# The first loads of a fused attention and feed-forward kernel: whole transfers for three groups and two weight slices, and another order of the opening

## The chip, the cores and the metric

The kernel runs on one core of one Trainium2 chip. The metric is the device time of one execution in microseconds (us); the median of three runs of the kernel before is 591.53 us (591.43 to 591.8). One more execution was recorded by the hardware profiler.

## The reference

`x` is the output of a chunked attention, and a gated feed-forward layer follows it. Cut to what matters:

```python
# q, k, v: (4, 8, 768, 64); mem_k, mem_v: (4, 8, 8, 64); chunks of 32, 16 to the left, 8 to the right
for c in range(nc):
    k_full = concat([mem_k, k[:, :, l_start:r_end]])      # 8 + up to 56 rows
    v_full = concat([mem_v, v[:, :, l_start:r_end]])
    scores = scale * (q_c @ k_full.T)
    a = exp(scores - max(scores))
    a = a / (sum(a) + 1e-09)
    out[:, :, c_start:c_end] = a @ v_full
x = out.transpose(0, 2, 1, 3).reshape(3072, 512)
h = x @ w_in                                              # (512, 2048)
g = where(h >= 1, h, where(h <= -1, 0, (h + 1) ** 2 / 4))
return g @ w_out                                          # (2048, 512)
```

## The kernel before, in words

The 3072 tokens are done in six blocks of 512. A block's attention output, transposed, is `x` (a high part `xth` and a rest `xtl`); the 2048 hidden units are 16 slices of 128. For a slice, TensorE (PE) multiplies `w_in` and `x` in three products of high and low parts into PSUM (a "hid" step, tile `ps_h`), ScalarE (ACT) and VectorE (DVE) form the gate (`gw`) and split it (`gh`, `gl`), and PE multiplies it by `w_out` into four accumulators (an "out" step, tile `ps_o`).

Weights arrive as raw 64-bit words, 16 pieces of 1024 KB, `w0` to `w15`, and are decoded on the chip by `decode` (line 160): ACT activates (`w`), DVE shifts and ors (`f`), ACT casts the high part, DVE subtracts for the low part (`wr`). The first two, `w0` and `w1`, are decoded in halves (`u0`, `u1` of `w0`; `u2`, `u3` of `w1`); before, each half also comes in a transfer of its own.

The attention of block 0 is done in four groups, g0 to g3 (`first_attention`, line 238). g0 and g1 make up the first 256 tokens, g2 and g3 the others. A group runs: scores on PE (`ps_s`), a mask memset where a window sticks out, maximum (`mx`), subtraction (`pr`), exponential on ACT, sum (`den`), `den + 1e-9`, reciprocal (`rin`), multiplication, four transposes on PE, two copies to `pt` on ACT, values on PE (`ps_x`), cast to `xth` on ACT, subtraction to `xtl` on DVE. g0 takes its maximum and subtraction in two halves; g2 does its exponentials in eight instructions with sums, and g3's scores take the PSUM banks that g2's scores leave. The mask of a group reads the scores of both halves of its queries and keys.

What sets the order around the change is a list written out in the kernel, the string `FIRST` (line 33). Each token advances one chain by one step, and each engine executes in program order. `L5` issues entry 5 of the list `loads` (line 646) on SP's queue; `g`, `u`, `w`, `n` are the chains named above (`n0` to `n3`: attention of later half blocks); `A0` to `A3` are the hid and out steps of slices 0 to 3 for the first 256 tokens, `B0` to `B3` those for the other 256, and `J4` onward the steps for all 512. C, D, E are block 1. The `ps_h` tiles rotate over two PSUM banks, so a hid step or a group's transposes wait until an earlier user of a bank has been read. From block 2 on, a plain loop follows.

Of the kernel before, what the change touches and what calls it, by code (L numbers as in the profile page):

```python
# [30 lines left out]


FIRST = """
    L2 L0 L1 g0 g0 g0 L3 g1 g0 g0 g1 g0 g0 g1 L8 g0 L6 L5 g0 u0 g1 L10 g0 g0 g1 L9 g1 g1 u1 g2 L4 g1
    g1 u1 u0 u0 u2 g0 g2 g0 L12 u0 u0 g2 u2 u1 L13 g3 g2 g1 g0 u1 L7 g2 u2 g2 g0 g3 L11 L16 L14 g3
    L15 L30 g1 u2 g1 L17 g1 g2 g3 L19 A0 g2 A0 g3 g3 g3 u1 u3 g3 A1 A0 L18 g3 w2 g2 g3 u2 g3 u3 u3
    L25 L23 L20 L31 g2 g3 A0 A2 g2 w2 u3 g3 A1 w2 n0 A2 A1 B0 A1 w2 L29 L22 w3 B0 A1 A0 u3 L21 w2 B0
    w3 B0 w5 w3 L28 A2 L27 L26 L24 w3 L32 A0 A1 A3 w5 B1 A3 B0 w5 A3 A2 w3 A2 n0 w5 w4 B1 B1 w4 B0
    B1 B2 A2 B2 B1 B3 B1 B2 J4 B3 n0 n0 w4 w4 B2 A3 n0 w6 B3 w4 A3 B2 n0 J5 w5 A3 B2 B3 w9 J4 w6 J4
    n0 w6 w9 J4 J6 w6 J4 B3 J5 n0 J5 w7 B3 n0 w6 J7 J5 J4 w7 J6 n0 w8 w7 w7 J5 w7 w8 J6 n0 J5 w8 J8  # L40
    w11 J6 J7 J6 J7 w10 w9 n0 w8 J8 n0 n0 w12 w9 J7 J8 w8 w9 J8 J6 n0 n0 w11 w10 n0 J7 n0 w10 w10
    J10 w11 J9 J9 w11 w13 w10 J8 w12 J9 J10 n1 n1 w11 J7 n1 w12 J10 J9 J12 w12 n1 J10 w12 n1 w14 J10
    n1 J9 w14 n1 w14 J8 J11 J9 J12 w13 J12 n1 w14 J11 J12 J13 J11 C0 w15 J12 J13 J11 w13 n1 n1 n1
    L34 L33 n2 J10 J11 n1 w13 C0 C0 w14 n1 J13 n1 C1 n2 C1 n2 n2 n2 C1 w15 C0 C1 J11 w13 J14 n2 J12
    w15 n2 C1 n2 C0 J13 J14 n1 J14 J14 L36 C2 J13 n1 C2 n1 C2 n2 J15 n2 J13 n1 n2 C3 w15 J14 L35 w15
    C2 J15 J14 n2 n2 J15 J15 C2 n2 n2 C3 D0 C3 J15 D1 D0 n2 n2 D1 C3 J15 n3 D0 J15 D1 n2 C3 n2 D2
    J15 n2 J15 D3 C0 C1 D3 D0 D2 n2 D3 n2 D0 D2 n3 n2 E5 D1 D3 n2 D2 E4 C2 n2 D3 D2 D1 E4 J15 E5 E4
    C3 n3 n3 E4 E6 E5 n3 n3 n3 E4 n3 D0 D1 E8 n3 D2 E5 D3 E6 E5 E6 E6 n3 E8 E4 E7 E6 n3 E8 E8 E7 E8
    n3 E5 E6 E7 E9 E10 L38 L37 E9 E7 E7 E9 E10 E10 n3 E7 E9 E9 n3 E13 E8 n3 E10 E12 E9 E10 E10 E12
    n3 E13 E12 n3 E13 E13 E13 E12 E11 E14 E11 E12 n3 n3 E11 n3 E14 E11 n3 E11 E15 E15 E14 E15 L39  # L50
    E11 n3 E12 E14 E14 n3 E15 n3 E15 E13
"""
# [784 lines left out]
```

## Time and profile before

| | |
|---|---|
| median of three runs | 591.53 us |
| profiled execution | 591.96 us |
| its span (first to last instruction) | 590.1 us |
| PE busy | 574.4 us, 97% |
| DVE busy | 332.2 us, 56% |
| ACT busy | 267.7 us, 45% |
| bytes read | 47.84 MB |

The span is what the instructions cover; 1.86 us of the profiled execution lie around it. "Busy" is time in which an engine has an instruction in hand. Every instruction of the kernel carries the line of one helper (L72), so rows are told apart by engine and tile.

### The profile page before, as it was taken

The numbers are of one execution on the slowest core, as the hardware profiler recorded it, in microseconds if no ns is written. First come the engines' busy times: TensorE is split into PE (matmuls) and PEld (weight loads), VectorE is DVE, ScalarE is ACT, GpSimd is POOL, SyncE is SP. The second block draws the span as 40 slices with busy tenths as digits, with TensorE's granted clock in tenths as the row PEclk, the third lists the DMA queues.
The fourth block names the chain that finished last, engine by engine and source line by source line (L and its number), as shares of the span: only waits on it lengthen the run. The fifth ranks groups of instructions, "written<-read, shape, count | busy, mean of one in ns | idle before, by whom it ended". The sixth has DMA issues, their size and how long they took to land.

```text
span 590.1 us, 12043 instructions
## 1 busy us (share of the span) xinstructions
PE 574.4 (97%) x5364; PEld 474.8 (80%) x5364; DVE 332.2 (56%) x489; ACT 267.7 (45%) x468; POOL 2.4 (0%) x7
## 2 busy tenths in 40 slices
...
DMA packets 10709, 54.91 MB, mean 93 GB/s; under 512 B 1185, under 2 KB 1185, under 8 KB 6305
## 3 DMA queue, kind: packets, MB, share of 16 engines
...
q8 instruction: 42, 0.69, 0.5%
...
HBM read 47.84 MB, written 6.29 MB: 92 GB/s over the span
## 4 chain that ended last, share of the span: by engine, by line
PE 85%; DVE 6%; ACT 5%; DMA 1%; issue 1%; SPq 0%; DVEq 0%; ACTq 0%
PE ps_o L72 41%; PE ps_h L72 40%; PE ps_x L72 2%; PE ps_s L72 2%; ACT pr L72 2%; DMA w<-in_first_w_dram 1%; DVE pt L72 1%; DVE f L72 1%; ACT gw L72 1%; ACT f L72 1%; DVE mx L72 1%; DVE gw L72 1%; DVE gl L72 1%; DVE wr L72 1%; ACT w L72 1%
## 5 line engine op out<-in xcount | busy, mean ns | idle before, releaser
L72 PE MATMUL ps_h<-xth,wr 128*128 128x512 f32 (+1 forms) x832 | 195.4, 376 | 1.2 <-ACT pt L72 0.6
L72 PE MATMUL ps_o<-wr,gh 128*128 128x512 f32 x768 | 194.5, 390 | 0.0
L72 PEld LDWEIGHTS ps_h<-xth,wr 128*128 128x128 f32 x832 | 147.5, 188 | 31.6 <-DVE wr L72 0.9
L72 PEld LDWEIGHTS ps_o<-wr,gh 128*128 128x128 f32 x768 | 143.5, 188 | 29.6
L72 DVE SCALAR_TENSOR_TENSOR gw<-ps_h,gw 128x512 f32<-128x512 f32 (+1 forms) x104 | 67.4, 648 | 141.1 <-ACT gw L72 140.4
L72 ACT ACTIVATE gw<-ps_h 128x512 f32<-128x512 f32 (+1 forms) x104 | 58.6, 564 | 178.1 <-PE ps_h L72 173.1
L72 PE MATMUL ps_o<-wr,gl 128*128 128x512 f32 x384 | 106.9, 389 | 0.0
L72 PE MATMUL ps_h<-xtl,wr 128*128 128x512 f32 (+1 forms) x416 | 104.5, 373 | 0.0
L72 DVE TENSOR_TENSOR gl<-gw,gh 128x512 fp32r<-128x512 f32 (+1 forms) x104 | 66.8, 647 | 54.4 <-ACT gh L72 53.8
L72 ACT CAST gh<-gw 128x512 fp32r<-128x512 f32 (+1 forms) x104 | 60.6, 587 | 65.6 <-DVE gw L72 55.6
L72 PEld LDWEIGHTS ps_h<-xtl,wr 128*128 128x128 f32 x416 | 75.0, 188 | 13.9
L72 PEld LDWEIGHTS ps_o<-wr,gl 128*128 128x128 f32 x384 | 72.1, 188 | 15.0
L72 ACT ACTIVATE gw<-gw 128x512 f32<-128x512 f32 (+1 forms) x104 | 62.3, 599 | 3.3
L72 DVE STREAM_TRANSPOSE pt<-pr 32x512 f32<-32x512 f32 (+1 forms) x60 | 41.4, 699 | 1.2
L72 DVE STREAM_TRANSPOSE xt<-xr 32x512 f32<-32x512 f32 (+1 forms) x48 | 33.1, 700 | 6.6 <-ACT xr L72 6.0
L72 ACT ACTIVATE pr<-pr 128x1024 f32<-128x1024 f32 (+1 forms) x12 | 11.4, 952 | 33.2 <-DVE pr L72 33.2
...
L72 DVE COPY ob<-ps_o 128x512 f32<-128x512 f32 (+1 forms) x16 | 9.6, 622 | 23.4 <-PE ps_o L72 23.3
L72 DVE SCALAR_TENSOR_TENSOR f<-w,f 128x1024 uint32<-128x1024 uint32 (+1 forms) x18 | 19.5, 1090 | 3.6 <-ACT f L72 3.4
L72 DVE TENSOR_TENSOR wr<-f,wr 128x1024 fp32r<-128x1024 f32 (+1 forms) x18 | 19.5, 1095 | 1.0 <-ACT wr L72 1.0
L72 ACT CAST wr<-f 128x1024 fp32r<-128x1024 f32 (+1 forms) x18 | 17.0, 951 | 5.9 <-DVE f L72 5.8
...
## 6 DMA issues: line engine op xcount, KB each, us to landing
...
```

The source lines that it names most:

```text
L72: return self.tc.keep_in_program_order(getattr(self.engine, name)(*args, **kwargs))
```

## The change

Groups 1, 2 and 3 get their queries and keys in one transfer each (672 KB) where there were two of 336 KB, and `w0` and `w1` come in one transfer of 1024 KB each where there were two of 512 KB. Group 0 keeps its two halves. Five entries of `loads` become `None`, so the numbers of the others stay. `FIRST` is replaced by another order of the same steps, without the five. `decode` and its halves are as they were.

```diff
 FIRST = """
-    L2 L0 L1 g0 g0 g0 L3 g1 g0 g0 g1 g0 g0 g1 L8 g0 L6 L5 g0 u0 g1 L10 g0 g0 g1 L9 g1 g1 u1 g2 L4 g1
-    g1 u1 u0 u0 u2 g0 g2 g0 L12 u0 u0 g2 u2 u1 L13 g3 g2 g1 g0 u1 L7 g2 u2 g2 g0 g3 L11 L16 L14 g3
-    L15 L30 g1 u2 g1 L17 g1 g2 g3 L19 A0 g2 A0 g3 g3 g3 u1 u3 g3 A1 A0 L18 g3 w2 g2 g3 u2 g3 u3 u3
-    L25 L23 L20 L31 g2 g3 A0 A2 g2 w2 u3 g3 A1 w2 n0 A2 A1 B0 A1 w2 L29 L22 w3 B0 A1 A0 u3 L21 w2 B0
...
+    L0 L1 L2 g0 g0 g0 g0 g1 g0 L5 g0 g1 g0 g0 u0 u0 g1 g1 u1 u0 g0 g0 u0 g1 L8 g1 g1 u1 g1 g0 L10
+    L12 g2 g0 u2 g2 u0 u2 g1 L7 g2 g3 g1 u2 u1 u1 g3 g2 g3 g2 L4 g1 u3 g3 u2 g1 g2 g3 g0 L15 L16 g2
+    g3 g1 g3 L14 g0 g0 L30 g2 g3 u2 u3 L20 u1 A0 g3 g3 w2 g2 g3 L19 u3 w2 A0 A1 A0 g3 g2 L17 A2 L18
+    g3 u3 A1 n0 w2 A2 L22 L23 L24 A0 g2 A2 A1 w6 w2 u3 A0 A1 B0 B0 A0 w5 A2 w2 A3 B0 B1 w3 A2 w5 A1
...
+        if g > 0:
+            sp.dma_start(qk_of[0, g], next_qk[g - 1])
+            return
         at = slice(r * QKF, (r + 1) * QKF)
-        sp.dma_start(qk_of[0, g][:, at], first_qk[g, r])
+        sp.dma_start(qk_of[0, g][:, at], first_qk[r])
...
-    def load_w(i, part=None):
+    def load_w(i):
...
-        if part is None:
-            sp.dma_start(raw[i], w[i - len(SLICED)].bitcast(U32))
-        else:
-            sp.dma_start(raw[i][:, part * n2 : (part + 1) * n2], first_w[i, part].bitcast(U32))
+        sp.dma_start(raw[i], w[i].bitcast(U32))
...
     loads = [
-        (load_first_qk, 0, 0), (load_first_qk, 0, 1), (load_first_qk, 1, 0), (load_first_qk, 1, 1),
-        (load_first_v, 0), (load_w, 0, 0), (load_w, 0, 1), (load_first_v, 1),
-        (load_first_qk, 2, 0), (load_first_qk, 2, 1), (load_w, 1, 0), (load_w, 1, 1),
-        (load_first_qk, 3, 0), (load_first_qk, 3, 1), (load_first_v, 2), (load_first_v, 3),
+        (load_first_qk, 0, 0), (load_first_qk, 0, 1), (load_first_qk, 1, 0), None,
+        (load_first_v, 0), (load_w, 0), None, (load_first_v, 1),
+        (load_first_qk, 2, 0), None, (load_w, 1), None,
+        (load_first_qk, 3, 0), None, (load_first_v, 2), (load_first_v, 3),
     ]
```

In the two orders, VectorE's first instructions are these (the step's name behind the group's, as in the section on the kernel; `shl`, `or`, `lo` are the steps of a decode, `eps` is `den + 1e-9`):

```
before: g0.mx g0.sub g0.mx g0.sub g1.mx g0.den g1.sub g0.eps g0.rin g0.mul g1.den g1.eps g1.rin g1.mul
        u1.shl u0.shl u0.or g2.mx u0.lo u2.shl u1.or g2.eps g2.rin u2.or g2.mul g0.lo g3.mx g3.sub g1.lo
        g3.den g3.eps g3.rin u1.lo g3.mul A0 u2.lo u3.shl u3.or g2.lo w2.shl g3.lo w2.or A1 ...
after:  g0.mx g0.sub g0.mx g0.sub g1.mx g0.den g0.eps u0.shl g1.sub u0.or g0.rin g0.mul g1.den g1.eps g1.rin
        u1.shl g1.mul g2.mx u0.lo u2.shl u2.or u1.or g3.mx g2.eps g3.sub g2.rin g2.mul g3.den g3.eps g1.lo
        g3.rin g0.lo g3.mul u2.lo u3.shl u1.lo u3.or w2.shl A0 g3.lo w2.or g2.lo A2 A1 ...
```

TensorE's, up to the same set of steps done:

```
before: g0 scores, g1 scores, g0 transposes, g2 scores, g1 transposes, g0 values, g3 scores, g1 values,
        g2 transposes, A0 hid, A1 hid, g3 transposes, g2 values, g3 values, A2 hid, n0 scores, B0 hid, ...
after:  g0 scores, g1 scores, g0 transposes, g2 scores, g1 transposes, g3 scores, g1 values, g0 values,
        g2 transposes, A0 hid, g3 transposes, g2 values, g3 values, A1 hid, A2 hid, n0 scores, B0 hid, ...
```

## Rows read from the trace of the kernel before

**Rows 1.** The page: its first line and section 1 (busy time, share of the span, instructions).

```profile
span 590.1 us, 12043 instructions
PE 574.4 (97%) x5364; PEld 474.8 (80%) x5364; DVE 332.2 (56%) x489; ACT 267.7 (45%) x468; POOL 2.4 (0%) x7
```

**Rows 2.** Busy time of the engines by stretch: stretch, its length, busy us (and instructions) of each engine, granted TensorE clock, DMA share, GB/s.

```profile
0.00:28.00 28.00, 17.46 (x396) 12.94 (x396) 18.74 (x42) 16.72 (x40) 2.44 (x7) 1.00 0.95 371
...
33.00:60.00 27.00, 27.00 (x145) 23.04 (x145) 25.92 (x39) 23.44 (x38) 0.00 (x0) 1.00 1.01 421
...
110.00:130.00 20.00, 19.43 (x223) 16.68 (x222) 14.16 (x23) 12.22 (x37) 0.00 (x0) 1.00 0.16 55
130.00:200.00 70.00, 70.00 (x689) 58.45 (x689) 33.36 (x53) 26.80 (x50) 0.00 (x0) 1.00 0.19 69
```

**Rows 3.** The chain that ended last, in order of time: start, duration, what.

```profile
16.59 2.48 ACT pr L72 x16
...
28.12 1.15 PE ps_x L72 x32
29.27 1.63 PE ps_h L72 x12
30.90 1.41 PE ps_s L72 x91
```

**Rows 4.** SP's queue in order of time: start of the issue, duration, tile. From the ninth issue on, SP issues a transfer when the one eight places earlier has landed.

```profile
6.54 0.33 SPq L72 DMA_DIRECT2D qk<-in_first_qk_dram  x1
...
7.87 0.33 SPq L72 DMA_DIRECT2D qk<-in_first_qk_dram  x1
...
9.95 0.33 SPq L72 DMA_DIRECT2D w<-in_first_w_dram  x1
11.22 0.33 SPq L72 DMA_DIRECT2D w<-in_w_dram  x1
...
13.26 1.18 SPq L72 DMA_DIRECT2D v<-in_first_v_dram  x2
...
15.43 0.33 SPq L72 DMA_DIRECT2D qk<-in_qk_dram  x1
...
17.02 0.33 SPq L72 DMA_DIRECT2D w<-in_w_dram  x1
...
19.53 0.33 SPq L72 DMA_DIRECT2D w<-in_w_dram  x1
...
27.81 0.33 SPq L72 DMA_DIRECT2D w<-in_w_dram  x1
```

**Rows 5.** Time from issue to landing of the first transfer (issued at 0.73) and of the second (issued at 1.16), one answer each.

```profile
DMA to landing us min/median/max: 3.1/3.1/3.1
...
DMA to landing us min/median/max: 3.5/3.5/3.5
```

**Rows 6.** Stretches of one microsecond; the last two columns are the DMA share and GB/s.

```profile
4.00:5.00 1.00, 0.32 (x24) 0.32 (x32) 0.00 (x0) 0.00 (x0) 0.00 (x0) 1.00 1.23 328
5.00:6.00 1.00, 0.37 (x31) 0.13 (x11) 0.00 (x0) 0.00 (x0) 0.00 (x0) 1.00 0.73 180
```

**Rows 7.** TensorE in order of time: start, duration, operation, tile, count, and in brackets the idle time before it and what ended it.

```profile
4.68 0.68 PE L72 MATMUL ps_s<-qk 64*32 64x64 f32 x32 [1.61 <-DMA qk<-in_first_qk_dram]
6.56 1.18 PE L72 MATMUL ps_s<-qk 64*32 64x64 f32 x64 [1.19 <-DMA qk<-in_first_qk_dram]
...
12.41 1.08 PE L72 MATMUL ps_h<-ident,pr 128*128 128x128 f32 x4 [3.84 <-DVE pr L72]
...
15.80 1.85 PE L72 MATMUL ps_x<-pt,v 128*64 128x64 f32 x32
19.12 0.86 PE L72 MATMUL ps_s<-qk 64*32 64x64 f32 x64 [1.48 <-ACT pr L72]
21.25 0.66 PE L72 MATMUL ps_h<-ident,pr 128*128 128x128 f32 x4
...
32.24 1.22 PE L72 MATMUL ps_h<-xth,wr 128*128 128x256 f32 x8
```

**Rows 8.** VectorE and ScalarE in order of time, the same columns.

```profile
7.38 0.11 DVE L72 MEMSET ps_s<- 32x64 f32 x1 [6.26 <-PE ps_s L72]
...
9.35 0.69 DVE L72 TENSOR_REDUCE mx<-ps_s 128x8 f32<-128x512 f32 x1
...
9.96 0.68 DVE L72 TENSOR_REDUCE den<-pr 128x8 f32<-128x512 f32 x1
...
11.23 0.66 ACT L72 ACTIVATE w<-w 128x512 f32<-128x512 f32 x1 [1.37 <-DMA w<-in_first_w_dram]
...
11.58 0.69 DVE L72 TENSOR_TENSOR pr<-pr,rin 128x512 f32<-128x512 f32 x1
...
15.61 0.68 DVE L72 TENSOR_REDUCE mx<-ps_s 128x8 f32<-128x512 f32 x1
...
17.12 0.43 DVE L72 TENSOR_SCALAR f<-w 128x512 uint32<-128x512 uint32 x1
...
18.92 1.19 ACT L72 COPY pt<-ps_h 64x512 f32<-64x512 f32 x2
```

**Rows 9.** What TensorE waited for between 100 and 135 us: us in total, times, longest.

```profile
PE ps_h L72 <- DVE gw L72: 0.4, 1, 0.4
PE ps_x L72 <- ACT pr L72: 0.2, 1, 0.2
```

More of the change, by code (lines that the diff above doesn't have):

```diff
@@ L33 @@
 FIRST = """
-    L2 L0 L1 g0 g0 g0 L3 g1 g0 g0 g1 g0 g0 g1 L8 g0 L6 L5 g0 u0 g1 L10 g0 g0 g1 L9 g1 g1 u1 g2 L4 g1
-    g1 u1 u0 u0 u2 g0 g2 g0 L12 u0 u0 g2 u2 u1 L13 g3 g2 g1 g0 u1 L7 g2 u2 g2 g0 g3 L11 L16 L14 g3
-    L15 L30 g1 u2 g1 L17 g1 g2 g3 L19 A0 g2 A0 g3 g3 g3 u1 u3 g3 A1 A0 L18 g3 w2 g2 g3 u2 g3 u3 u3
-    L25 L23 L20 L31 g2 g3 A0 A2 g2 w2 u3 g3 A1 w2 n0 A2 A1 B0 A1 w2 L29 L22 w3 B0 A1 A0 u3 L21 w2 B0
-    w3 B0 w5 w3 L28 A2 L27 L26 L24 w3 L32 A0 A1 A3 w5 B1 A3 B0 w5 A3 A2 w3 A2 n0 w5 w4 B1 B1 w4 B0
@@ L39 @@
[L39 to L48, printed above, removed]
@@ L49 @@
-    n3 E5 E6 E7 E9 E10 L38 L37 E9 E7 E7 E9 E10 E10 n3 E7 E9 E9 n3 E13 E8 n3 E10 E12 E9 E10 E10 E12
-    n3 E13 E12 n3 E13 E13 E13 E12 E11 E14 E11 E12 n3 n3 E11 n3 E14 E11 n3 E11 E15 E15 E14 E15 L39
-    E11 n3 E12 E14 E14 n3 E15 n3 E15 E13
+    L0 L1 L2 g0 g0 g0 g0 g1 g0 L5 g0 g1 g0 g0 u0 u0 g1 g1 u1 u0 g0 g0 u0 g1 L8 g1 g1 u1 g1 g0 L10
+    L12 g2 g0 u2 g2 u0 u2 g1 L7 g2 g3 g1 u2 u1 u1 g3 g2 g3 g2 L4 g1 u3 g3 u2 g1 g2 g3 g0 L15 L16 g2
+    g3 g1 g3 L14 g0 g0 L30 g2 g3 u2 u3 L20 u1 A0 g3 g3 w2 g2 g3 L19 u3 w2 A0 A1 A0 g3 g2 L17 A2 L18
@@ new lines @@
+    g3 u3 A1 n0 w2 A2 L22 L23 L24 A0 g2 A2 A1 w6 w2 u3 A0 A1 B0 B0 A0 w5 A2 w2 A3 B0 B1 w3 A2 w5 A1
+    w3 A3 A1 A3 B1 B0 B2 w3 B0 B1 w4 w3 w5 w3 B0 B3 A3 L25 L21 B2 n0 A2 B3 B1 B2 w4 B2 L26 L32 L27
+    B1 L31 A3 w4 J4 L28 n0 B3 w5 w4 J4 B3 L29 w4 n0 B2 B3 w8 B1 w7 J4 w5 n0 J5 w6 w6 J4 J5 J5 J4 n0
+    w6 B2 w8 n0 w6 J6 J6 B3 A3 J5 J5 w7 J6 w11 w8 w8 J7 J7 n0 w7 n0 J4 J6 w9 J5 n0 n0 w7 w10 J6 w7
+    n0 n0 n0 J8 w10 n0 w8 J7 w12 w10 w9 n0 J7 w9 n0 J7 L33 J9 J9 n0 w9 J9 J6 J8 n1 w9 w10 n1 w10 L34
@@ new lines @@
+    w13 J9 J8 w15 w11 w14 J7 n1 J9 w11 n1 J8 J10 w11 w11 J8 n1 J11 n1 J11 J10 J8 n2 n1 n1 J10 w12 J9
+    J12 n1 w12 n1 n2 J11 w12 w13 J11 J10 w13 w13 C0 J10 n1 w12 C0 w14 J10 n1 n1 J11 n1 w13 n2 C0 w15
+    J12 J11 J12 J13 J12 J12 C1 J13 C1 n2 C0 n2 n2 w15 J13 C1 J12 J13 n2 J13 w14 J14 C2 n1 C1 J14 w14
+    w14 C1 w15 C0 n2 C2 n2 C2 J14 J13 C3 n1 J14 C3 L36 L35 J15 w15 J14 J14 J15 n1 C3 n1 n2 n2 n2 J15
+    C3 J15 J15 n2 D0 J15 C2 D0 C2 C3 n2 n2 J15 D0 D1 E4 J15 D1 E4 n2 n2 D1 n2 n2 E4 C0 E4 C1 J15 J15
@@ L52 @@
+    D2 n2 E4 D3 n3 D2 D0 D3 D1 C2 D0 D3 C3 D0 E6 L37 D3 n3 D1 D2 n2 D2 E6 D3 n2 D1 E7 n2 E6 D2 E7 E6
+    E7 n2 n2 D2 D3 E5 n3 n3 E6 n3 E4 E5 E7 n3 E5 n3 n3 E7 E9 n3 E8 E5 n3 E9 E9 n3 n3 n3 E5 E8 E8 E12
+    E5 n3 n3 n3 E9 E9 E6 E10 E8 E10 E8 E12 E7 n3 E12 E10 E8 E10 E11 E13 n3 n3 E9 E10 E11 E11 E11 E14
+    E12 E11 n3 E12 E13 E10 E14 E14 E13 n3 E11 E15 E13 E13 n3 E12 E14 E15 E15 n3 E15 L38 n3 L39 E13
+    E14 E15
 """
@@ L77, in attn_ffn_kernel @@
 @with_exitstack
-def attn_ffn_kernel(ctx: ExitStack, tc: tile.TileContext, first_qk, first_v, qk, vw, first_w, w, out):
+def attn_ffn_kernel(ctx: ExitStack, tc: tile.TileContext, first_qk, next_qk, first_v, qk, vw, w, out):
     nc = tc.nc
@@ L81, in attn_ffn_kernel @@
     pe, act, dve, pool, sp = (InOrder(tc, e) for e in engines)
-    NP = first_qk.shape[0]
+    NP = next_qk.shape[0] + 1
     NM = 8
@@ L86, in attn_ffn_kernel @@
     DM = NP * P
-    NPW = len(SLICED) + w.shape[0]
+    NPW = w.shape[0]
     NFC = NPW
```

8 lines of the change are left out of this document (3 added, 5 removed).

## The prediction

> **What bounds the kernel now.** I read the page's busy times first: TensorE is busy 574.4 of 590.1 us [rows 1], so the end can move only by what TensorE idles, 15.7 us, or by a change of its work; the change leaves the work alone. The table by stretch then places the idle time [rows 2]: 10.5 us before 28 us, none from 33 to 60 and from 130 to 200, 0.57 between 110 and 130, where TensorE waits twice [rows 9]. So the question is when TensorE begins its unbroken run. The chain of waits [rows 3] answers: until 28.12 us it goes through ACT, DVE and DMA, from then on through PE: g3's values, A2's hid, n0's scores, B0's hid at 32.24 [rows 7]. The order after does the same set of steps before B0's hid (A1's hid only later), and if TensorE then stays unbroken, as it does now, the difference in B0's start is the difference in the end.
>
> **The loads.** SP's queue shows when each transfer lands, and bytes go out in issue order [rows 4, 5]: after 336 KB 3.83 us, 672 KB 4.68, 1008 KB 6.54, 1344 KB 7.87, 2192 KB (the first `w0` half) 9.95, 2704 KB 11.22, 3216 KB 13.26, 4064 KB 15.43, 4736 KB 17.02, 5760 KB 19.53. I keep this curve and read the new places off it. g0's halves come first and second, 3.83 and 4.68 (before 4.68 and 6.54). g1 whole ends at 1344 KB, 7.87, as now. `w0` whole ends at 2368 KB: 9.95 + 176/512 x 1.27 = 10.4, where its halves landed at 9.95 and 11.22. g2's whole ends at 3040 KB, about 12.55. `w1` whole ends at 4064 KB, 15.43, where the first half came at 13.26. g3's is at 17.02 as before; v0 moves back from 15.43 to 19.53, v1 is before it.
>
> Issuing: five issues fewer on SP save nothing, since from the ninth on SP waits for landings anyway [rows 4]. SP also has to wait before it issues `w9`, whose buffer the second decoded half of `w1` (`u3`) must leave (27.81 now [rows 4]); `w10`, `w11` and `w7` stand behind it in the new order. `w9` becomes the nineteenth issue; `w6`, `w5`, `w3`, `w4` and `w8` are in front of it, 2.5 us each at 421 GB/s [rows 2], so the queue has work until about 41 us and the stand costs nothing.
>
> **The opening, step by step.** g0's second scores start at 4.68 instead of 6.56, so the mask, which waits for both halves, goes from 7.38 to 5.50 [rows 7, 8]: 1.9 us gained. It is lost at once: DVE's next instruction in order is g1's maximum. g1's scores start at 7.87 and take 1.18 [rows 7]; with the mask of 0.15 the maximum begins at 9.35, as it does now [rows 8]. Behind it stands g0's `den`, 9.96, again as now. Now the orders part. Before, g0's multiplication came at 11.58 and its transposes at 12.41. After, `u0`'s shift stands in front of g1's subtraction, and it needs ACT's 0.66 us [rows 8] on `w0`: 10.40 + 0.66 + 0.03 = 11.09. From there at the rows' spacing (0.60 from one 512-column instruction to the next, 0.35 for a shift of 0.43): g1.sub 11.44, u0.or 12.04, reciprocal 12.64, g0.mul 12.86 to 13.55. **g0's transposes start at 13.69 instead of 12.41: 1.28 us late.** Bounds: had `w0` landed at 9.7 or earlier, 0.6 late; at the lag of the transfers after 11.22 (0.8 us more), 2.0 late.
>
> Then: transposes 1.08, g2's scores 1.18, to about 15.95; g2.mx 16.05 (before 15.61 [rows 8]); the eight exponentials, 0.98 behind it, 17.03 + 2.48 [rows 3] = 19.51 (before 19.07). Only 0.44 is left of the delay, since g2's scores no longer wait for a second half. g3's scores need g2's banks: 19.56 to 20.42. DVE: g3.mx 20.5, g3.sub 21.21, g2.mul 22.03, g3.den 22.63, g1.lo 23.6, g0.lo 24.4, g3.mul 24.95 to 25.63. ACT: pt of g1 until 20.62 (1.19 a pair [rows 8]), g3.exp to 22.55, highs of g1 and g0 until 24.1, pt of g2 to 25.2. PE: g1's and g0's values after 20.67 (1.15 each [rows 3]; v0 has landed at 19.53), g2's transposes 22.9, A0's hid 24.13 to 25.65, g3's transposes 25.77 (0.66 [rows 7]), ACT's pt 26.4 to 27.57, g3's values 27.6 to 28.75. That is 0.5 earlier than now (29.27), but A1's hid, done by then in the old order, is still to come: + 1.6. A2's hid 1.63, n0's scores 1.41: 33.35; B0's hid waits for the gates of A1 and A2 on ACT and DVE to be read, about 33.5. **Sum: 33.5 - 32.24 = + 1.25 us.**
>
> Of the steps behind, I followed the same way which is last up to n0's values near 71 us: `w2`'s low part 0.1 before use, A1's `gl` 0.4 before, `w4`'s low part 0.7 before its use in J5. DVE is busy 25.9 of 27 us from 33 to 60 [rows 2], so these margins are thin; I charge nothing for them, and up to 1.0 at the upper bound. Later waits of the old order, 0.6 [rows 9], may go or come: bounds -0.6 and +0.6, value 0.
>
> **A second term: TensorE's speed.** The granted clock reads 1.00 throughout [rows 2], yet 32 value products took 1.85 us at 15.80 [rows 7] and 1.15 at 28.12 [rows 3], 64 score products 1.18 at 6.56 and 0.86 at 19.12 [rows 7]: by durations, the lower level until some 17 us, after TensorE had worked without a break since 12.41. In the new order it works from 13.69 to 17.1 and then stands 2.4 us for g2's exponentials, where the old order had g0's values. If it is still at the lower level at 19.56, g3's scores take 0.3 more, g1's and g0's values 0.7 more each; g0's cast then begins at 24.45 instead of 23.5, A0's hid at 25.1 instead of 24.13, and g3's transposes behind A0 at 26.9 instead of 25.77: + 1.15. Bounds 0 and 1.15 (2 if A0 ran at that level too). I take 0.5, since the work before the gap is 1.3 us shorter than the 4.7 that preceded the rise. The Trainium skill, TensorE: Matmul & The Clock Gate, section "What's actually happening", says that the slow rate is the default, that sustained activity lifts it, and that the looking is not tied to the kernel's start. The trace agrees as to the first two; by that rule this term would differ from run to run, between the two bounds.
>
> **Result.** 591.96 for the profiled execution + 1.25 + 0.5 = 593.7; the median of the runs is 0.43 below that execution, so 593.3 us.
>
> **The rivals.**
> (a) The head of the stream speeds up. From 4 to 6 us it carried 328 and 180 GB/s [rows 6] against 421 later [rows 2]; the sum of what is missing is (421 - 328 + 421 - 180)/421 = 0.8 us. If that dip comes from the many small transfers being set up, it goes: g1 lands about 7.0, `w0` 9.4 to 9.6, g0's transposes come near 12.7, g2's exponentials end near 18.5, and B0's start is + 0.2 to + 0.4 late; without the 0.6 of [rows 9] the end is 0.2 to 0.4 earlier: 591.3, not slower. For it: the dip lies where eight transfers are queued at once. Against it: the halves of 336 and 512 KB that follow move at full rate. It decides from `w0` landing at 9.5 or earlier. The Trainium skill, DMA: Bandwidth & Descriptors, section "Rules for kernel authors", asks for transfers of 1 MiB and more and for small ones to be joined. By that rule (a) would be the likelier; the rows above show the rate of 421 GB/s with halves too.
> (b) The low level stays and the thin margins break: 1.25 + 1.15 + about 1.0 where DVE is full (J5 and J8 hid waiting for low weights, n0's values for transposes) = + 3.4: 594.9. For it: DVE's 25.9 of 27. Against: TensorE too is later by the same amount, which widens the margins of what depends on DMA alone.
> (c) The new order is better past 33 us than I can follow by rows, and g0's early lead is kept (w0 at 9.7 and no slow clock: + 0.5, then - 0.6 and more for the late waits and for hid steps that follow score or value blocks): 590.7. Against it: TensorE is unbroken there, so there is little to win.
>
> **Chances.** Main case 0.52, with its own range 592.4 to 594.3; (a) 0.2; (b) 0.17; (c) 0.11. A measurement of this kernel tells 0.2%, 1.2 us, from no change. Slower by more: (b) and most of the main case (it holds + 0.9 to + 1.2 at its lower end), 0.17 + 0.43 = 0.60. Within: 0.09 of the main case, 0.17 of (a) and 0.02 of (c), 0.28. Faster: the other 0.09 of (c) and 0.03 of (a), 0.12. The range 590.6 to 595.2 leaves out about one tenth on either side.
>
> **What would show it.** In the profile after: g0's mask near 5.5, and g1's maximum again near 9.35 (a start before 8.7 speaks for (a)); ACT's first `w` near 10.4; g0's transposes near 13.7; the end of the eight exponentials near 19.5; value products at 20.7 of 1.15 us or 1.85; g3's values ending 28.7 to 29.9; B0's hid from 33.5 to 34.6; no waits of TensorE from there to 110. It is wrong if `w0` lands more than 0.7 us off 10.4, or if TensorE shows idle time between 34 and 110 us.

## The result, and the profile after

The median after is 594.76 us (594.10 to 595.72), beside 591.66 us (591.43 to 591.80) for the kernel before on the same chip: ratio 1.0053, 95% interval 1.0038 to 1.0068. The change makes the kernel 3.1 us slower. 593.3 us was forecast, with 590.6 to 595.2 as the range and slower as the likeliest sign. The profiled execution took 595.23 us. Of all runs in this document one, of e1 below, was far off (722.43 us); it is left out of e1's ratio, and without it e1's median would be 594.54.

The page of the kernel after, first line and busy times:

```profile
span 593.5 us, 12032 instructions
PE 575.7 (97%) x5364; PEld 475.5 (80%) x5364; DVE 332.4 (56%) x489; ACT 268.5 (45%) x468; POOL 2.4 (0%) x7
```

The busy times are those of [rows 1] but for 1.3 us more of TensorE and 0.8 of ScalarE, and the span is 3.4 us longer. So most of the loss, 2.1 us, is idle time of TensorE. The table by stretch of the kernel after, with the columns of [rows 2], says where:

```profile
0.00:28.00 28.00, 15.75 (x370) 12.02 (x372) 17.40 (x40) 14.60 (x36) 2.44 (x7) 1.00 0.95 383
...
33.00:60.00 27.00, 27.00 (x267) 23.03 (x267) 24.61 (x41) 22.74 (x40) 0.00 (x0) 1.00 1.01 421
60.00:110.00 50.00, 49.86 (x587) 40.98 (x586) 44.25 (x55) 37.49 (x55) 0.00 (x0) 1.00 0.33 121
110.00:130.00 20.00, 19.44 (x219) 16.26 (x218) 14.57 (x23) 14.46 (x46) 0.00 (x0) 1.00 0.15 55
```

TensorE is busy 1.7 us less before 28 us than it was. ScalarE has 46 instructions between 110 and 130 us, where it had 37, and is busy 2.2 us more. TensorE of the kernel after, in order of time:

```profile
3.68 1.51 PE L72 MATMUL ps_s<-qk 64*32 64x64 f32 x64 [0.61 <-DMA qk<-in_first_qk_dram]
8.36 1.19 PE L72 MATMUL ps_s<-qk 64*32 64x64 f32 x64 [3.17 <-DMA qk<-in_next_qk_dram]
14.12 1.09 PE L72 MATMUL ps_h<-ident,pr 128*128 128x128 f32 x4 [4.58 <-DVE pr L72]
...
16.25 1.11 PE L72 MATMUL ps_h<-ident,pr 128*128 128x128 f32 x4
19.93 1.18 PE L72 MATMUL ps_s<-qk 64*32 64x64 f32 x64 [2.56 <-ACT pr L72]
21.04 3.68 PE L72 MATMUL ps_x<-pt,v 128*64 128x64 f32 x64
...
25.41 1.21 PE L72 MATMUL ps_h<-xth,wr 128*128 128x256 f32 x8
...
28.87 1.15 PE L72 MATMUL ps_x<-pt,v 128*64 128x64 f32 x32 [0.24 <-ACT pt L72]
...
34.47 1.22 PE L72 MATMUL ps_h<-xth,wr 128*128 128x256 f32 x8
```

The last row is B0's hid: 34.47 against 32.24 [rows 7], **2.23 us late**. The last matmul starts at 588.48, before at 585.28: 3.20 late. So 0.97 more is lost behind B0's hid. The value products at 21.04 took 1.84 us for each 32, the lower level; the granted clock reads 1.00 all the same. VectorE and ScalarE of the kernel after:

```profile
5.34 0.11 DVE L72 MEMSET ps_s<- 32x64 f32 x1 [4.21 <-PE ps_s L72]
...
9.77 0.69 DVE L72 TENSOR_REDUCE mx<-ps_s 128x8 f32<-128x512 f32 x1
...
10.82 0.65 ACT L72 ACTIVATE w<-w 128x512 f32<-128x512 f32 x1 [3.00 <-DMA w<-in_w_dram]
...
11.51 0.43 DVE L72 TENSOR_SCALAR f<-w 128x512 uint32<-128x512 uint32 x1 [0.25 <-ACT w L72]
11.85 0.69 DVE L72 TENSOR_TENSOR pr<-ps_s,mx 128x512 f32<-128x512 f32 x1
...
13.28 0.69 DVE L72 TENSOR_TENSOR pr<-pr,rin 128x512 f32<-128x512 f32 x1
...
17.40 0.32 ACT L72 ACTIVATE pr<-ps_s,mx 128x64 f32<-128x64 f32 x1 [0.22 <-PE ps_h L72]
```

The chain of the prediction stands in these rows: g0's mask at 5.34 instead of 7.38 [rows 8]; no use of it at g1's maximum (9.77); `w0` at 10.82; `u0`'s shift at 11.51 in front of g1's subtraction; g0's multiplication at 13.28; its transposes at 14.12. Last, what TensorE of the kernel after waited for between 34 and 135 us, with the columns of [rows 9]:

```profile
PE ps_h L72 <- DVE gw L72: 0.3, 1, 0.3
PE ps_o L72 <- ACT wr L72: 0.2, 1, 0.2
```

The instructions of TensorE in order of time, around these waits:

```profile
105.56 1.07 PE L72 MATMUL ps_o<-wr,gl 128*128 128x512 f32 x4
106.77 2.11 PE L72 MATMUL ps_h<-xth,wr 128*128 128x512 f32 x8
...
120.30 2.45 PE L72 MATMUL ps_o<-wr,gh 128*128 128x512 f32 x8 [0.18 <-ACT wr L72]
122.59 1.08 PE L72 MATMUL ps_o<-wr,gl 128*128 128x512 f32 x4
123.98 1.22 PE L72 MATMUL ps_h<-xth,wr 128*128 128x256 f32 x8 [0.32 <-DVE gw L72]
```

The waits that the views name come to 0.5 us, no more than the 0.6 of [rows 9]; they are at other places. One more gap is too short to be named: 0.14 us between the rows at 105.56 and 106.77. So the waits alone do not explain the 0.97.

### The profile page after: what moved, and what is told of

The parts are those of the page before. It is cut to its first block, busy times and chain, and to the rows that moved or that the text cites. A ratio compares the mean times of both kernels' runs of the same rounds, so it can differ in the third digit from the quotient of the medians.

```text
span 593.5 us, 12032 instructions
## 1 busy us (share of the span) xinstructions
PE 575.7 (97%) x5364; PEld 475.5 (80%) x5364; DVE 332.4 (56%) x489; ACT 268.5 (45%) x468; POOL 2.4 (0%) x7
## 4 chain that ended last, share of the span: by engine, by line
PE 88%; ACT 5%; DVE 4%; DMA 1%; issue 1%; SPq 0%; DVEq 0%; ACTq 0%
PE ps_h L72 43%; PE ps_o L72 40%; PE ps_x L72 3%; PE ps_s L72 2%; DMA w<-in_w_dram 1%; ACT pr L72 1%; ACT gw L72 1%; DVE gl L72 1%; ACT wr L72 1%; ACT w L72 1%; DVE wr L72 1%; ACT gh L72 1%; DVE pt L72 1%; DVE pr L72 1%; DVE f L72 0%
## 5 line engine op out<-in xcount | busy, mean ns | idle before, releaser
L72 DVE STREAM_TRANSPOSE xt<-xr 32x512 f32<-32x512 f32 (+1 forms) x48 | 33.0, 699 | 10.4 <-ACT xr L72 9.7
L72 ACT ACTIVATE w<-w 128x1024 f32<-128x1024 f32 (+1 forms) x18 | 18.6, 1038 | 3.0 <-DMA w<-in_w_dram 3.0
```

What stands on the lines that cost most here:

```text
L72: return self.tc.keep_in_program_order(getattr(self.engine, name)(*args, **kwargs))
```

## The experiments

Each kernel was timed at least five times (the kernel after four times; e7, e11 and e12 eleven times) beside the kernel before, whose median was 591.65 to 591.87 us. "B0" is the start of B0's hid, "stretch" the time from there to the start of the last matmul, both in the profiled execution.

| kernel | median us | ratio, 95% interval | B0 | stretch |
|---|---|---|---|---|
| before | 591.66 | | 32.24 | 553.04 |
| after | 594.76 | 1.0053 (1.0038 to 1.0068) | 34.47 | 554.01 |
| e1_u0_behind | 594.61 | 1.0049 (1.0036 to 1.0063) | 34.53 | 553.74 |
| e2_whole_old_order | 593.86 | 1.0042 (1.0030 to 1.0055) | 34.54 | 553.06 |
| e3_new_order_halves | 593.56 | 1.0033 (1.0020 to 1.0045) | 33.37 | 553.71 |
| e4_work_in_gap | 594.77 | 1.0053 (1.0040 to 1.0067) | 34.30 | 553.80 |
| e5_g0_values_in_gap | 594.18 | 1.0036 (1.0023 to 1.0049) | 33.67 | 553.75 |
| e6_work_from_start | 595.31 | 1.0052 (1.0040 to 1.0065) | 33.18 | 554.45 |
| e7_old_g0_first | 591.71 | 0.9998 (0.9989 to 1.0006) | 31.90 | 553.06 |
| e9_w14_first | 595.30 | 1.0051 (1.0038 to 1.0065) | 34.85 | 553.82 |
| e10_w14_early | 596.23 | 1.0079 (1.0066 to 1.0092) | 35.27 | 554.74 |
| e11_halves_new_order_values_in_gap | 592.79 | 1.0016 (1.0007 to 1.0025) | 32.16 | 553.78 |
| e12_whole_qk_only | 592.23 | 1.0007 (0.9998 to 1.0015) | 32.46 | 553.07 |
| e13_new_opening_old_rest | 593.95 | 1.0042 (1.0029 to 1.0056) | 32.26 | 555.00 |

**The transfers alone.** The old order with all five transfers whole, against the kernel before:

```diff
-    L2 L0 L1 g0 g0 g0 L3 g1 g0 g0 g1 g0 g0 g1 L8 g0 L6 L5 g0 u0 g1 L10 g0 g0 g1 L9 g1 g1 u1 g2 L4 g1
+    L0 L1 L2 g0 g0 g0 g1 g0 g0 g1 g0 g0 g1 L8 g0 L5 g0 u0 g1 L10 g0 g0 g1 g1 g1 u1 g2 L4 g1
```

> The order of steps of the kernel before, with the whole transfers (loads in the old sequence, each pair joined; g0's halves first). Theory (whole transfers alone already cost, since w0 and w1 land later than their first halves did): w0 lands near 12.5, w1 near 15.5, g2's exponentials start near 17.9 instead of 16.6, and the time is + 1.0 to + 1.8 against the kernel before. Rival 1 (the cost is in the new order alone): within 0.5 us of the kernel before. Rival 2 (fewer, larger transfers run faster): w0 lands before 12 and the time is under the kernel before.

2.2 us slower, and B0 2.30 late. ScalarE of this kernel:

```profile
13.06 0.67 ACT L72 ACTIVATE w<-w 128x512 f32<-128x512 f32 x1 [4.94 <-DMA w<-in_w_dram]
13.63 0.61 ACT L72 ACTIVATE pr<-pr 128x512 f32<-128x512 f32 x1
...
18.43 0.31 ACT L72 ACTIVATE pr<-ps_s,mx 128x64 f32<-128x64 f32 x1 [0.25 <-DVE mx L72]
```

ScalarE takes its instructions in order, and the activation of `w0` stands in front of g1's exponential. That exponential now waits for the whole of `w0`, and everything of g1 and g2 behind it comes later: g2's exponentials start 1.84 us after those of [rows 3]. Behind B0 nothing more is lost (553.06). To part the two kinds of transfer, the next kernel has only the queries and keys whole (and the old list without `L3`, `L9` and `L13`):

```diff
-        sp.dma_start(qk_of[0, g][:, at], first_qk[g, r])
+        if g > 0:
+            sp.dma_start(qk_of[0, g], next_qk[g - 1])
+            return
+        sp.dma_start(qk_of[0, g][:, at], first_qk[r])
```

> The kernel before with its own order; only the queries and keys of groups 1 to 3 come in whole transfers, w0 and w1 stay in halves. With all five transfers whole, the old order takes 2.2 us more, and B0's hid starts 2.3 us later; its trace shows ScalarE waiting for the whole of w0 in front of g1's exponential. Theory: all of that is w0's; then here ScalarE's first activation of w0 starts at 11.2 to 11.5 us, g2's exponentials near 16.6, B0's hid at 32.0 to 32.5, and the time is within 0.3 us of the kernel before. Rival: the queries and keys have a share, since the scores of a group's first half can't start before all of it has landed (g1's and g2's scores); then g2's exponentials start 0.3 to 1 us later, and the time is 0.5 to 1.2 us above the kernel before.

ScalarE of this kernel, the same two instructions:

```profile
11.40 0.66 ACT L72 ACTIVATE w<-w 128x512 f32<-128x512 f32 x1 [1.05 <-DMA w<-in_first_w_dram]
...
16.82 0.31 ACT L72 ACTIVATE pr<-ps_s,mx 128x64 f32<-128x64 f32 x1 [0.25 <-DVE mx L72]
```

Its median is 0.4 us above the kernel before, on an interval that reaches from just under no change to 0.9 us; `w0`'s activation is back at 11.40, beside 11.23 [rows 8]. This lies between the theory's edge (0.3) and the rival's (0.5), so a small share of the queries and keys stays possible. But some 1.8 of the 2.2 us come with the whole weights (g0's halves first, which e2 has and this kernel has not, cost nothing in e7 below).

In the old order a whole `w0` is not late because its other half has to come too: in the kernel before, the half that is decoded first is issued second (`L6 L5`), so its activation at 11.23 [rows 8] also had all of `w0` in front of it. And in e2 as in e12 the transfers up to the end of `w0` come to 3040 KB; whole it is in by 13.06, in halves by 11.39. The stretch up to there, with the columns of [rows 2], in e2:

```profile
0.00:13.06 13.06, 4.43 (x132) 2.25 (x132) 4.74 (x13) 1.91 (x3) 2.45 (x7) 1.00 0.86 315
```

And in e12:

```profile
0.00:11.39 11.39, 4.19 (x132) 2.26 (x132) 3.66 (x10) 1.91 (x2) 2.44 (x7) 1.00 0.85 310
```

An estimate from these rates: 4020 KB had been moved in e2 and 3450 in e12, so 980 KB of transfers issued later were through before the whole `w0` was in, and 410 before its halves were. The difference of 570 KB is 1.4 us at the 421 GB/s of [rows 2], most of the 1.67 us between the two landings. Bytes do not go out strictly in issue order here, and with the larger transfers more of the later ones went ahead. (The new order issues first the half that is decoded first. In e3 below it is in at 9.12, the whole of `w0` in the kernel after at 10.82, so there the other half's time is lost as well.)

**The order alone.** The new order with the half transfers of before:

```diff
-    L0 L1 L2 g0 g0 g0 g0 g1 g0 L5 g0 g1 g0 g0 u0 u0 g1 g1 u1 u0 g0 g0 u0 g1 L8 g1 g1 u1 g1 g0 L10
+    L0 L1 L2 L3 g0 g0 g0 g0 g1 g0 L5 L6 g0 g1 g0 g0 u0 u0 g1 g1 u1 u0 g0 g0 u0 g1 L8 L9 g1 g1 u1 g1
```

> The new order of steps and loads, each whole transfer split in its two halves again, issued one after the other. Theory (the new order alone costs, by g0's values moved out of the stretch from 15.8 to 17.6 and TensorE's low level after the gap): w0's first half lands near 9.5, g0's transposes start near 13.3, g3's scores and the value products behind still run at the low level, and the time is + 1.5 to + 2.7 against the kernel before. Rival 1 (only the whole transfers cost): within 0.5 us of the kernel before. Rival 2 (low level by chance of the run): value products of 1.15 us in this profile and a spread of over 1 us between the runs.

1.9 us slower with the old transfers. g2's exponentials start at 16.17, 0.42 earlier than in [rows 3], yet B0 is 1.13 late, and 0.67 is lost behind it. So both parts of the change are dear by themselves, and together they cost less (3.1) than the sum of the two (4.1): with whole transfers the new order loses 0.9 more than the old one, with halves 1.9.

**The wait for `u0`'s shift.** The prediction's 1.28 us. In the new order, VectorE:

```diff
-g0.eps u0.shl g1.sub u0.or g0.rin g0.mul g1.den
+g0.eps g1.sub g0.rin g0.mul u0.shl u0.or g1.den
```

> The changed kernel with two tokens moved: u0's shift and or stand behind g0's multiplication again. Theory (part of the loss is the order on DVE: g0's multiplication waits for w0 through u0's shift): g0's transposes start near 12.8 instead of 14.12, the eight exponentials of g2 end near 19.0 instead of 19.9, and the time is 0.9 to 1.3 us under the changed kernel's 594.8, so + 1.8 to + 2.2 against the kernel before. Rival 1 (only TensorE's level counts): transposes earlier, but the gap in front of g3's scores is as long, the value products still take 1.85 us, and the end is within 0.3 us of 594.8. Rival 2 (the loss lies behind 34 us): no change at the end.

TensorE of this kernel in order of time, g0's and g1's transposes:

```profile
13.32 1.09 PE L72 MATMUL ps_h<-ident,pr 128*128 128x128 f32 x4 [3.29 <-DVE pr L72]
...
16.31 1.09 PE L72 MATMUL ps_h<-ident,pr 128*128 128x128 f32 x4 [0.80 <-DVE pr L72]
```

And ScalarE's first exponential of g2:

```profile
17.44 0.31 ACT L72 ACTIVATE pr<-ps_s,mx 128x64 f32<-128x64 f32 x1 [0.76 <-PE ps_h L72]
```

g0's transposes come 0.80 earlier (13.32), and the time does not move. A part of that is the landings of this execution: g1 is in at 8.82 and `w0` at 11.30, 0.5 later than in the kernel after. Counted from g1's landing, the transposes gain 1.29, as forecast, but the exponentials only 0.45. ScalarE's row says why: g2's exponentials wait for a `ps_h` of TensorE, the end of g1's transposes, since g2's probabilities are written to the buffer (`tag="pr"`) that g1's transposes read. Those transposes wait for g1's multiplication, and the steps of `u0`, moved behind g0's, now stand in front of that one. The prediction followed g2's exponentials through their maximum alone and did not see this second condition. In the kernel after it costs nothing yet, since the maximum is ready at 17.25 and the transposes end at 17.36; here they end at 17.40, and the maximum is ready at 16.97. A gain of 0.45 in the time is within the intervals of the two medians, so it is neither shown nor excluded.

**TensorE's level in the gap.** Six products of a tile of zeros, which nothing reads, behind g1's transposes; the kernel computes the same:

```diff
-    L12 g2 g0 u2 g2 u0 u2 g1 L7 g2 g3 g1 u2 u1 u1 g3 g2 g3 g2 L4 g1 u3 g3 u2 g1 g2 g3 g0 L15 L16 g2
+    L12 g2 g0 u2 g2 u0 u2 g1 k6 L7 g2 g3 g1 u2 u1 u1 g3 g2 g3 g2 L4 g1 u3 g3 u2 g1 g2 g3 g0 L15 L16
...
+    def warm_step(n):
+        keep_warm(n)
+        yield
```

> The changed kernel with six extra products of the zero tile behind g1's transposes, whose result nobody reads, in the gap in which TensorE stands for g2's exponentials (17.4 to 19.9). Theory (TensorE's low level after the gap costs 1.0 us or more): the level rises in the gap or soon after it, g1's and g0's value products take 1.15 us each instead of 1.85, B0's hid starts near 33.4 instead of 34.47, and the time is 1.0 us (0.7 to 1.3) under the changed kernel's. Rival (the level costs nothing, as ACT and DVE set the path): value products are shorter but the end is within 0.3 us of 594.8.

TensorE of this kernel in order of time:

```profile
21.17 2.08 PE L72 MATMUL ps_x<-pt,v 128*64 128x64 f32 x64 [0.19 <-ACT pt L72]
...
24.75 1.10 PE L72 MATMUL ps_h<-xth,wr 128*128 128x256 f32 x7 [0.72 <-ACT xth L72]
26.06 0.39 PE L72 MATMUL ps_h<-xth,wr 128*128 128x256 f32 x1 [0.22 <-issue]
...
34.30 1.22 PE L72 MATMUL ps_h<-xth,wr 128*128 128x256 f32 x8
```

The level rises: 64 value products take 2.08 us, not 3.68, and A0's hid starts at 24.75, not 25.41. But B0 gains 0.17 and the time nothing. Part of the rest goes to a stall in A0's hid: from its first product to its `xtl` part 1.54 us pass (24.75 to 26.29), 1.05 in the kernel after. The view gives it as "issue", which only the two kernels with added products show. The stall makes 0.49, and the exponentials start 0.18 later here (17.58). So the price of the low level stays open between 0.17 and the sum of the three, 0.84. With products from the start (five, nine and six behind g0's scores, g1's scores and g1's transposes) the level is high from the first transposes on:

```diff
-    L0 L1 L2 g0 g0 g0 g0 g1 g0 L5 g0 g1 g0 g0 u0 u0 g1 g1 u1 u0 g0 g0 u0 g1 L8 g1 g1 u1 g1 g0 L10
+    L0 L1 L2 g0 k5 g0 g0 g0 g1 k9 g0 L5 g0 g1 g0 g0 u0 u0 g1 g1 u1 u0 g0 g0 u0 g1 L8 g1 g1 u1 g1 g0
```

> The changed kernel with extra products of the zero tile behind g0's scores (5), behind g1's scores (9) and behind g1's transposes (6), so that TensorE works nearly without a break from 3.7 us. Theory (TensorE's level counts where its three blocks run back to back in front of g2's exponentials, 14.1 to 17.4): the blocks take 2.2 us instead of 3.26, the exponentials end near 18.9 instead of 19.9, the value products take 1.15, B0's hid starts near 33.2, and the time is 1.0 to 1.4 us under the changed kernel's. Rival (u2's decode on w1 and g2's maximum come at the same moment as the end of g1's transposes): the exponentials start only 0.2 us earlier and the time stays within 0.3 us.

TensorE of this kernel, behind B0's hid:

```profile
36.61 0.40 PE L72 MATMUL ps_o<-wr,gh 128*128 128x512 f32 x1 [1.03 <-issue]
```

B0 comes 1.29 us earlier, but a stall of the same kind, 1.03 us long, follows at 36.61, and the stretch is 0.44 longer than in the kernel after. The runs lie from 594.18 to 595.82, the median is no better than the kernel after. So added work raises the level and brings its own stalls; for the time this test is inconclusive.

**g0's values back in the gap.** The new order with whole transfers; g0's values, cast and low part as early as before, and `v0`'s load ahead of g3's:

```diff
-PE: g1.tr g3.sc g1.val g0.val g2.tr
+PE: g1.tr g0.val g3.sc g1.val g2.tr
-ACT: g2.exp g1.pt u1.hi u3.act g3.exp u2.hi g1.hi g0.hi g2.pt
+ACT: g2.exp g0.hi g1.pt u1.hi u3.act g3.exp u2.hi g1.hi g2.pt
-DVE: u1.or g3.mx ... g3.rin g0.lo g3.mul
+DVE: u1.or g0.lo g3.mx ... g3.rin g3.mul
-SP: L10 L12 L7 L4
+SP: L10 L4 L12 L7
```

> The changed kernel with g0's values, cast and rest back in the gap in which TensorE stands for g2's exponentials (as in the order before), and with v0's load in front of g3's and v1's so that it lands in time (near 17). Theory (part of the loss in the opening is that g0's values stand behind the gap, at TensorE's low level): the gap of 2.6 us in front of g3's scores shrinks under 1, A0's hid starts near 24.4 instead of 25.4, B0's hid near 33.5 instead of 34.5, and the time is 0.8 to 1.2 us under the changed kernel's 594.8. Rival (g3's chain on DVE and ACT is as long): A0's hid earlier, but g3's transposes still near 26.9 and the end within 0.3 us of 594.8.

B0 0.80 earlier, median 0.6 lower, without a product added. g3's scores and g1's values run at the high level (0.86 and 1.15 us, from 20.04), and g3's transposes now wait for VectorE (0.19 at 26.10), so TensorE has no more to give there. The same edit on top of the half transfers (in its list, too, `v0`'s load `L4` stands ahead of g3's, `L12 L13`, and behind g2's, unlike what the expectation says):

> The new order with the half transfers, and with g0's values back in the gap behind g1's transposes (g0's cast and low part moved up with them, v0's load ahead of g2's). The new order with halves alone starts B0's hid at 33.37 us (before: 32.24) and takes 1.9 us more than the kernel before; with whole transfers the same move of g0's values gave 0.80 us at B0's hid and 0.6 us of time. Theory: what the new order loses in the opening with half transfers is g0's values at the low level behind the gap and A1's hid behind g3's values; with the values back B0's hid starts at 32.3 to 32.7, and the time is 1.0 to 1.4 us above the kernel before, of which 0.7 is the late loss of the new order. Rival: the opening is bound by VectorE's and ScalarE's steps behind g2's exponentials, whatever TensorE does in the gap; then B0's hid starts at 33.1 or later and the time is 1.7 us or more above the kernel before.

TensorE of this kernel, g0's values and B0's hid:

```profile
16.26 1.44 PE L72 MATMUL ps_x<-pt,v 128*64 128x64 f32 x32 [0.28 <-DMA v<-in_first_v_dram]
...
32.16 1.22 PE L72 MATMUL ps_h<-xth,wr 128*128 128x256 f32 x8
```

B0 stands at 32.16, 0.08 earlier than before: the opening's loss is gone (g2's exponentials start 0.57 earlier than in [rows 3], at 16.02, and the steps behind them take 0.49 more). The time is still 0.9 us above the kernel before, and the stretch 553.78 instead of 553.04. That is the later loss by itself.

**The later loss.** The kernels so far that have the new list's later steps, and no products added, take 553.7 to 554.0 us from B0 to the last matmul; those with the old order take 553.0 to 553.1. Three edits look for it. First, VectorE's or-instructions of `w14` and `w15` exchanged:

```diff
-J12.gl w15.or J13.gate C1.gate n2.eps J13.gl w14.or w14.lo
+J12.gl w14.or J13.gate C1.gate n2.eps J13.gl w15.or w14.lo
```

> The changed kernel with two VectorE steps exchanged far behind the opening: the or of w14 in front of that of w15, since J13's out step needs w14 first. Theory (the loss behind 34 us, 1.0 in the profile and 0.7 in the other runs of the new order, lies in the new order's later waits, first of all at 120 us where TensorE waits for w14's high part): the waits at 118 to 124 us, 1.2 us in all, shrink by half or more, and the time is 0.4 to 0.8 us under the changed kernel's. Rival (DVE is late for all of them alike): the wait goes to J14's out step, and the time stays within 0.2 us.

No change (the waits are at 120.65 and 124.34): the high part of `w14` is cast on ScalarE at 119.22 in the kernel after, and ScalarE is the one that is late, behind n2's exponentials (until 116.5), two casts and a gate. So, second, that cast ahead of most of n2's exponentials, with the or and the low part earlier on VectorE:

```diff
-ACT: C1.gate n2.exp C0.gh n2.exp n2.exp J13.gh C1.gh J14.gate w14.hi w15.hi
+ACT: C1.gate w14.hi n2.exp C0.gh n2.exp n2.exp J13.gh C1.gh J14.gate w15.hi
-DVE: C0.gate J12.gate J12.gl w15.or J13.gate C1.gate n2.eps J13.gl w14.or w14.lo C1.gl
+DVE: C0.gate w14.or J12.gate J12.gl w15.or w14.lo J13.gate C1.gate n2.eps J13.gl C1.gl
```

> The new order as it is, with three steps of w14's decode earlier: its or on VectorE behind w15's shift, its cast to the high part on ScalarE ahead of the second of n2's four runs of exponentials, its low part on VectorE behind w15's or. The kernel after starts B0's hid at 34.47 us and ends 554.0 us later; every kernel of the new order takes 553.7 to 554.0 for that stretch, the kernel before 553.05. In the trace after, TensorE waits near 120.5 for ScalarE's high part of w14 (0.2) and near 124 for a gate (0.3). Theory: part of the late loss is that ScalarE does w14's cast behind n2's exponentials; then both waits go, the stretch from B0's hid to the last matmul is 0.3 to 0.6 us shorter, and the time 594.2 to 594.5. Rival: the waits are only where a shortage shows that lies in VectorE's and ScalarE's whole load before 125 us; then they come back a few us later (at J14's or J15's out, or at n1's values) and the stretch stays within 0.15 us of 554.0, the time within 594.5 to 595.3.

TensorE of this kernel, the one wait that is left there:

```profile
116.56 2.11 PE L72 MATMUL ps_h<-xth,wr 128*128 128x512 f32 x8 [1.79 <-DVE gw L72]
```

VectorE of this kernel just before:

```profile
114.68 1.22 DVE L72 TENSOR_TENSOR wr<-f,wr 128x1024 fp32r<-128x1024 f32 x1 [1.91 <-ACT wr L72]
115.82 1.01 DVE L72 SCALAR_TENSOR_TENSOR gw<-ps_h,gw 128x512 f32<-128x512 f32 x2
```

Both waits go, and a larger one comes: the low part waits 1.91 us for ScalarE's cast, and the gates that TensorE waits for stand behind it on VectorE. The stretch grows by 0.73, where neither theory had it. (Of its time, 1.5 us above the kernel after, 0.8 is at B0 already, where nothing differs: `w0` landed at 11.46 in this execution.) Third, e11's opening and, from B0 on, the old order:

```diff
 FIRST: e11's order up to B0's hid
-... then e11's remaining steps
+... then the remaining steps in the order of before
```

> Half transfers and the new order's opening with g0's values in the gap (as in the kernel whose B0's hid starts at 32.16 us and whose time is 0.93 us above the kernel before), and from B0's hid on the remaining steps in the order of the kernel before. From B0's hid to the last matmul that kernel takes 553.78 us, the kernel before 553.04. Theory: the late loss lies in the new order's steps behind B0's hid; then the stretch takes 553.0 to 553.2 us, B0's hid starts at 32.1 to 32.4, and the time is within 0.4 us of the kernel before. Rival: the late loss comes from what VectorE and ScalarE have done and not done when B0's hid starts (eight steps more, among them w6's activation, and ScalarE's order until then); then the stretch takes 553.5 us or more, and the time is 0.6 us or more above the kernel before.

ScalarE of this kernel, its activation of `w3`:

```profile
35.53 1.13 ACT L72 ACTIVATE w<-w 128x1024 f32<-128x1024 f32 x1 [1.19 <-DMA w<-in_w_dram]
```

And TensorE's longest wait behind B0:

```profile
42.15 1.22 PE L72 MATMUL ps_h<-xth,wr 128*128 128x256 f32 x8 [0.71 <-DVE gw L72]
```

B0 is at 32.26, and the stretch 555.0: worse than either order. The rival had this: the rest depends on what the opening leaves behind. The new opening loads `w6` and `w5` ahead of `w3`; the old rest wants `w3` next, ScalarE waits 1.19 us for it with gates queued behind, and TensorE waits for these gates. So this run does not tell whether the 0.7 lies in the later steps by themselves; the old opening with the new rest was not tried. Last, the one gain that the new list brings, g0's halves first, in the kernel before, and with it the half of `w0` that is decoded first in front of the other:

```diff
-L2 L0 L1 L3 L8 L6 L5 L10
+L0 L1 L2 L3 L8 L5 L6 L10
```

> The kernel before with two pairs of loads exchanged: g0's halves in front of g1's first half (the one gain that the change has in the opening), and of w0 the half that is decoded first in front of the other. Theory (in the old order the path to g2's exponentials runs over w0's landing at 11.22 and ACT's order, so the change's early g0 could pay there): w0's first half lands near 9.9, g2's exponentials start near 16.0 instead of 16.6, B0's hid 0.4 to 0.7 us earlier, and the time is 0.3 to 0.7 us under the kernel before. Rival (w1's landing at 13.3 and g1's transposes hold g2 anyway): within 0.2 us of it.

That half of `w0` is in at 10.18, 1.0 us earlier than before; B0 comes 0.34 earlier in the profile, and the time is the same. No version tried beats the kernel before.

## Why the prediction was right, and where it was off

**The sign and the mechanism** hold: TensorE's unbroken run begins later, and the end follows. The forecast for the profiled execution was 593.7 us; it took 595.23. The 1.5 us between have these places. The median, 594.76, lies above the main case's own range, 592.4 to 594.3, and inside the whole one, 590.6 to 595.2, in the part that stands for (b).

**The landings.** `w0` was put at 10.4 and ScalarE starts on it at 10.82; g1's were put at 7.87, and SP's queue of the kernel after has them at 8.33:

```profile
8.33 0.33 SPq L72 DMA_DIRECT2D w<-in_w_dram  x1
10.82 0.33 SPq L72 DMA_DIRECT2D v<-in_first_v_dram  x1
```

The step that read the new places off the old curve of bytes is 0.4 us short, within the 0.7 that the prediction allowed itself. That it came so near is in part luck, since its premise, "bytes go out in issue order", does not hold. The stretches up to these two landings in the kernel after:

```profile
0.00:8.33 8.33, 3.25 (x68) 1.30 (x68) 1.99 (x6) 1.91 (x2) 2.44 (x7) 1.00 0.79 290
0.00:10.82 10.82, 4.43 (x132) 2.25 (x132) 3.16 (x9) 1.91 (x2) 2.44 (x7) 1.00 0.84 320
```

And up to the landings of the same bytes in e3, the same order with half transfers:

```profile
0.00:7.88 7.88, 3.93 (x100) 1.75 (x100) 1.99 (x6) 1.91 (x2) 2.45 (x7) 1.00 0.75 241
0.00:10.38 10.38, 4.62 (x132) 2.19 (x132) 3.57 (x11) 2.57 (x3) 2.45 (x7) 1.00 0.82 283
```

An estimate from these rates: when g1 (1344 KB) and `w0` (2368 KB) were in, 1010 KB of later transfers had been moved too, where e3 has 510 and 500. Some 500 KB more are 1.2 us at 421 GB/s, and the faster head of the stream gave 0.8 of that back. From 10.82 on, the forecast's steps fit: g0's transposes 3.30 us later (forecast 3.29), the exponentials' end at 19.88 (19.51), B0 at 34.47, where 33.5 and the level's 0.5 make 34.0.

**"g0's transposes start at 13.69 instead of 12.41"** is right but for the landing, and was not the whole price. e1 takes it back and gains 0.45 at the exponentials and nothing that the runs show, because g2's exponentials also wait for g1's transposes to leave the `pr` buffer. e2 shows the other half of the story: the old order pays for the whole `w0` too, through ScalarE.

**The level.** The products at 21.04 are at the lower level, as in the upper bound (1.84 us, forecast 1.85 or 1.15). The Trainium skill, TensorE: Matmul & The Clock Gate, section "What's actually happening", has the slow rate as the default and sustained activity as what lifts it; e4 and e6 agree (2.08 us for 64 products once the gap has work in it). That the level differs from run to run, which the prediction drew from the same section, holds in the small: at 21 us of the kernel after and at the same step of e1, e3, e9 and e10 the 64 products took 3.68 each time, but the rise behind them moves. e9 does the same steps as the kernel after until 110 us, and its A0's hid is still slow:

```profile
25.49 1.47 PE L72 MATMUL ps_h<-xth,wr 128*128 128x256 f32 x8
```

In the kernel after it took 1.21 at 25.41. B0 of e9 comes 0.38 later (34.85), of which the exponentials (17.47) account for 0.07. The 0.5 lies between the 0.17 and 0.84 that e4 leaves open. What e5 and e11 show is a price of the order: with g0's values behind the gap, 0.8 us at B0 with whole transfers and 1.2 with halves (0.9 and 1.1 from the start of g2's exponentials on). The level has a part in it, since with the values in the gap g3's scores and g1's values run at the high level.

**"These margins are thin; I charge nothing for them"** is the step that failed: the end is 0.97 later than B0 alone would make it. Where the block loop repeats the same steps, the kernel after is 2.95 late at 233.00 (the same step starts at 230.05 before); so 0.72 is lost by then, and the last 0.25 in the loop itself. e11 has 0.74 at that place and 0.74 at the end, and e1, e3, e5 and e9 lose 0.67 to 0.78 in all, so the 0.25 is of one execution, the 0.7 of the new order. By the gaps between TensorE's rows, 105 to 125 us has about 0.3 to 0.4 of it; there n2's exponentials, `w14`'s decode and gates crowd ScalarE. Where the rest of the 0.7 lies stays open. The line "no waits of TensorE from there to 110" is wrong as well, by the 0.14 us at 106.6; idle time between 34 and 110 us was one of the prediction's own signs of being wrong.

**The rivals.** (a) is half right: the stretch from 4 to 6 us now moved 379 and 393 GB/s instead of 328 and 180 [rows 6], as it said, but what was gained were bytes of later transfers, and g1 and `w0` landed later than forecast, not earlier. The Trainium skill, DMA: Bandwidth & Descriptors, section "Rules for kernel authors", wants small transfers joined; the rate did rise there, but a `w0` joined to 1024 KB landed 1.67 us later in e2 than its two halves in e12. (b) gave 594.9, nearest to the measured time: its two sums, 2.4 in the opening and 1.0 behind it, are what was seen (2.23 and 0.97). Its causes are so in part only: the low level did stay, but where the forecast has 1.15 for it, the 0.98 seen is made of 0.4 of landing and a rest that e4 lets the level explain, and what has been found of the late loss is at 105 to 125 us, not at J5, J8 or n0's values. That its sums come out is in part luck. (c) falls: from B0 on the new order loses 0.7 to 1.0.
